# Attention backward on one core: transposing loads with 16 source rows instead of 32, and a third buffer for two stored tiles

## The chip, the cores and the metric

The kernel runs on one core of a Trainium2 chip. The metric is the time of one execution in microseconds (us) on the device. Single executions of one kernel spread by 1 to 2% here, so every comparison below is made on one chip, in alternating rounds. A quoted ratio is the mean time of one kernel's fast runs over that of the kernel before in the same rounds, so it is not quite the ratio of the medians that are quoted beside it. "Faster" means by more than 2%.

## The reference

Two independent attention blocks (A and B) and their gradients. For each block:

```
q      = (x @ wq) in 32 heads of 128            x: 8 x 96 x 640
scores = q k^T * 128^-0.5                       k_cache, v_cache: 8 x 32 x 512 x 128
p      = softmax(scores);  o = p v;  out = o @ wo
outputs: out of both blocks, and the gradients of x, k, v, wq, wo of each
```

Everything is bf16. The large tensors are K, V and their gradients dK, dV: per batch element and pair of heads, 256 KB each.

## The kernel before

The work is cut into 256 batch steps: 2 blocks x 16 head pairs x 8 batch elements. Each step needs K and V in two layouts, so it loads them twice: once plainly (V2, K2) and once transposed by the DMA (KT2, VT2), with the head dimension on the partitions. It stores dV and dK. That is six DMAs of 256 KB per step, all issued in program order by SP (the SyncE).

```python
def ldKT(hp, b):                                     # ldVT is alike, from vc, as VT2
    t_ = kvp.tile([128, RG, 32], BF16, name="KT2", bufs=3)            # RG = 512 / 16
    nc.sync.dma_start_transpose(t_[:], kc[b, 2*hp:2*hp+2].rearrange("h (r g) d -> (h r) (g d)", r=16))
...
def key_order(ap):   # the order of keys that the transpose leaves -> the order of the plain tiles
    return ap.rearrange("q (s c r) -> q c r s", c=KC, r=16)           # KC = 4
...
# cS: scores of head i. cDP does the same with VT into dP_ps.
nc.tensor.matmul(S_ps[:, i, :], hs["QT"][:, i, tok], st["KT"][:, :, i*16:(i+1)*16], start=True, stop=True)
...
# cE reads S_ps through key_order (exp, ACT); cDP's last step reads dP_ps so (DVE)
...
# cDV; cDK is alike with dS, Qnat, dK_sb, dk
... 8 matmuls into v_ps (one PSUM buffer, shared by cDV and cDK)
o = wk.tile([128, 2, KC * 128], BF16, name="dV_sb", bufs=2)
evac("act", o[:], v_ps[:])                                            # line 68, on ACT
nc.sync.dma_start(dv[b, 2*hp:2*hp+2].rearrange("h (p c) d -> p h (c d)", c=KC), o[:])
```

With `r=16` the source of a transpose is 32 rows (16 per head) of 8 KB. The rest of the work of a head pair (projections, dwq, dwo, dx) is spread over the steps.

Of the kernel before, what the change touches and what calls it, by code (L numbers as in the profile page):

```python
# [11 lines left out]
BF16 = mybir.dt.bfloat16  # L12
# [22 lines left out]
def build_block(tc, em, tick0, blk, x, kc, vc, wq, wo, g_all, out_all, dx, dk, dv, dwq, dwo, ident, ones, pools, first, GP):  # L35
    nc = tc.nc
# [6 lines left out]
    KC = Sk // 128  # L43
# [7 lines left out]
    RG = Sk // 16  # L51
# [8 lines left out]
    const, ps, psS, psV, kvp, wk, hd, hst, stp = (pools[k] for k in ("const", "ps", "psS", "psV", "kv", "wk", "hd", "hst", "stp"))  # L60
    S, G, HS, CS = {}, {}, {}, {}

    def bank(shape, dt, name):
        return ps.tile(shape, dt, name=name, tag="bank")

    def evac(eng, dst, src, sc=None):
        if eng == "act":
            nc.scalar.activation(dst, src, ACT.Identity, scale=(1.0 if sc is None else sc))  # L68
        elif sc is None:
            nc.vector.tensor_copy(dst, src)  # L70
        else:
            nc.vector.tensor_scalar(dst, src, float(sc), None, op0=ALU.mult)
# [98 lines left out]

    def ldKT(hp, b):
        def f():
            t_ = kvp.tile([128, RG, 32], BF16, name="KT2", bufs=3)
            nc.sync.dma_start_transpose(t_[:], kc[b, 2 * hp:2 * hp + 2].rearrange("h (r g) d -> (h r) (g d)", r=16))
            CS[(hp, b)] = dict(KT=t_)
        return f

    def ldVT(hp, b):
        def f():  # L180
            t_ = kvp.tile([128, RG, 32], BF16, name="VT2", bufs=3)
            nc.sync.dma_start_transpose(t_[:], vc[b, 2 * hp:2 * hp + 2].rearrange("h (r g) d -> (h r) (g d)", r=16))
            CS[(hp, b)]["VT"] = t_
        return f

# [12 lines left out]
        return f  # L198

    def key_order(ap):  # L200
        return ap.rearrange("q (s c r) -> q c r s", c=KC, r=16)

    def c_major(ap):
        return ap.rearrange("q (c r s) -> q c r s", c=KC, r=16)

    def cS(hp, b):
        def f():
            st, hs = CS[(hp, b)], HS[hp]
            tok = slice(b * Sq, (b + 1) * Sq)
            S_ps = psS.tile([Sq, 2, Sk], F32, name="S_ps", bufs=1)  # L210
            for i in range(2):
                nc.tensor.matmul(S_ps[:, i, :], hs["QT"][:, i, tok], st["KT"][:, :, i * 16:(i + 1) * 16], start=True, stop=True)  # L212
            negm = wk.tile([Sq, 2], F32, name="negm", bufs=2)
            nc.vector.tensor_reduce(negm[:], S_ps[:], axis=AX.X, op=ALU.max, negate=True)  # L214
            st["S_ps"], st["negm"] = S_ps, negm
        return f

    def cE(hp, b):
        def f():
            st = CS[(hp, b)]  # L220
            E = wk.tile([Sq, 2, Sk], BF16, name="E_sb", bufs=2)
            rowsum = wk.tile([Sq, 2], F32, name="rowsum", bufs=2)
            for i in range(2):
                nc.scalar.activation(c_major(E[:, i, :]), key_order(st["S_ps"][:, i, :]), ACT.Exp, bias=st["negm"][:, i:i + 1], scale=1.0, accum_out=rowsum[:, i:i + 1])  # L224
            st["E"], st["rowsum"] = E, rowsum
        return f
# [30 lines left out]
    def cDV(hp, b):  # L257
        def f():
            st, hs = CS[(hp, b)], HS[hp]
            v_ps = psV.tile([128, 2, KC * 128], F32, name="v_ps", bufs=1)  # L260
            for i in range(2):
                for c in range(KC):
                    nc.tensor.matmul(v_ps[:, i, c * 128:(c + 1) * 128], st["P"][:, i, c * 128:(c + 1) * 128], hs["dOnat"][:, i, b * 128:(b + 1) * 128], start=True, stop=True)  # L263
            o = wk.tile([128, 2, KC * 128], BF16, name="dV_sb", bufs=2)
            evac("act", o[:], v_ps[:])
            nc.sync.dma_start(dv[b, 2 * hp:2 * hp + 2].rearrange("h (p c) d -> p h (c d)", c=KC), o[:])
        return f
# [23 lines left out]
    def cDP(hp, b):  # L291
        def f():
            st, hs = CS[(hp, b)], HS[hp]
            tok = slice(b * Sq, (b + 1) * Sq)
            dS = wk.tile([Sq, 2, Sk], BF16, name="dS_sb", bufs=2)
            dl_ps = bank([Sq, 2], F32, "dl_ps")
            dps = []
            for i in range(2):
                dP_ps = bank([Sq, Sk], F32, "dP_ps")
                nc.tensor.matmul(dP_ps[:], hs["dOT"][:, i, tok], st["VT"][:, :, i * 16:(i + 1) * 16], start=True, stop=True)  # L300
                nc.tensor.matmul(dl_ps[:, i:i + 1], st["prod"][:, i, :], ones[:, 0:1], start=True, stop=True)  # L301
                dps.append(dP_ps)
            for i in range(2):
                nc.vector.scalar_tensor_tensor(c_major(dS[:, i, :]), key_order(dps[i][:]), dl_ps[:, i:i + 1], c_major(st["P"][:, i, :]), op0=ALU.subtract, op1=ALU.mult)  # L304
            st["dS"] = dS
        return f
# [13 lines left out]
    def cDK(hp, b):  # L320
        def f():
            st, hs = CS[(hp, b)], HS[hp]
            v_ps = psV.tile([128, 2, KC * 128], F32, name="v_ps", bufs=1)
            for i in range(2):
                for c in range(KC):
                    nc.tensor.matmul(v_ps[:, i, c * 128:(c + 1) * 128], st["dS"][:, i, c * 128:(c + 1) * 128], hs["Qnat"][:, i, b * 128:(b + 1) * 128], start=True, stop=True)  # L326
            o = wk.tile([128, 2, KC * 128], BF16, name="dK_sb", bufs=2)
            evac("act", o[:], v_ps[:])
            nc.sync.dma_start(dk[b, 2 * hp:2 * hp + 2].rearrange("h (p c) d -> p h (c d)", c=KC), o[:])
        return f  # L330
# [254 lines left out]
```

## Time and profile before

| | before |
|---|---|
| median of the first 3 runs | 1821.9 us (1809.4 to 1822.78) |
| profiled execution | 1809.5 us |
| PE busy | 1647.6 us, 91% |
| time with at least 15 DMA packets in flight (packet records, 100 to 1700 us) | 95% |
| eviction of dV_sb to the issue of its store, median | 6.1 us |

The list of waits of the kernel before: who waited for whom, us in total, times, longest.

```profile
ACT dV_sb L68 <- DMA out_dram<-dV_sb: 86.0, 47, 8.0
...
ACT dK_sb L68 <- DMA out_dram<-dK_sb: 25.3, 17, 4.7
...
PE v_ps L326 <- ACT dV_sb L68: 96.9, 88, 8.0
```

A store has not landed; ACT cannot evict into its buffer; PE cannot reuse v_ps. It is the only large wait on PE.

Two groups that read through `key_order` (busy us, mean ns of one | idle before, releaser):

```profile
L224 ACT ACTIVATE E_sb<-S_ps,negm 96x512 bf16<-96x512 f32 x512 | 346.0, 681 | 186.8 <-DVE negm L214 184.6
...
L304 DVE SCALAR_TENSOR_TENSOR dS_sb<-dP_ps,dl_ps,P_sb 96x512 bf16<-96x512 f32 x512 | 361.3, 744 | 120.2 <-PE dl_ps L301 119.7
```

### The profile page before, as it was taken

How to read it: one execution, taken by the hardware profiler on the slowest of the kernel's cores; microseconds unless marked ns; L12 is line 12 of the kernel's file. 1: busy time of each engine (PE TensorE's matmuls, PEld its weight loads, DVE VectorE, ACT ScalarE, POOL GpSimd, SP SyncE). 2: the span in 40 equal slices, each digit the busy share in tenths (PEclk: the TensorE clock that was granted, in tenths of full speed). 3: DMA queues.
4: the chain of work that ended last, by engine and by line, in shares of the span. 5: the costliest groups of instructions: out<-in, count | busy, mean ns of one | idle time of the engine just before them, and what ended most of it. 6: DMA issues, size and time to landing. Idle time of an engine off the chain costs nothing. (4 is left out here: it accounts for less than half of the span.)

```text
span 1809.5 us, 51178 instructions
## 1 busy us (share of the span) xinstructions
PE 1647.6 (91%) x20061; PEld 1264.4 (70%) x20280; DVE 1244.8 (69%) x2069; ACT 1185.7 (66%) x2433; POOL 615.2 (34%) x930
## 2 busy tenths in 40 slices
PE   6889989988999999999978989899898998999998
PEld 4667767766777777677756767667676776777775
DVE  3767776766776776666756667666676776777774
ACT  3766666766676766666756667667676766776673
POOL 2333333332333333333334433233332333333333
PEclk9999999999999999999999999999999999999999
DMA  9999999999999999999999999999999999999995
GB/s 237 256 277 271 273 247 282 264 267 253 260 281 259 275 281 262 250 258 276 272 264 259 277 271 267 267 245 254 278 281 259 269 255 275 280 285 279 253 295 171
DMA packets 918002, 478.82 MB, mean 265 GB/s; under 512 B 643040, under 2 KB 906720, under 8 KB 917760
## 3 DMA queue, kind: packets, MB, share of 16 engines
q1 hardware_dynamic: 904224, 425.73, 103.0%
q0 software_dynamic: 13536, 49.82, 9.1%
q8 instruction: 158, 2.59, 0.6%
q14 instruction: 84, 0.69, 0.1%
HBM read 161.09 MB, written 159.12 MB: 177 GB/s over the span
## 5 line engine op out<-in xcount | busy, mean ns | idle before, releaser
L241 POOL TENSOR_SCALAR P_sb<-E_sb,rinv 96x512 bf16<-96x512 bf16 x512 | 348.4, 690 | 499.1 <-DVE rinv L232 496.4
L224 ACT ACTIVATE E_sb<-S_ps,negm 96x512 bf16<-96x512 f32 x512 | 346.0, 681 | 186.8 <-DVE negm L214 184.6
L304 DVE SCALAR_TENSOR_TENSOR dS_sb<-dP_ps,dl_ps,P_sb 96x512 bf16<-96x512 f32 x512 | 361.3, 744 | 120.2 <-PE dl_ps L301 119.7
L214 DVE TENSOR_REDUCE negm<-S_ps 96x2 f32<-96x1024 f32 x256 | 311.7, 1217 | 104.8 <-PE S_ps L212 104.5
L68 ACT ACTIVATE dK_sb<-v_ps 128x1024 bf16<-128x1024 f32 x256 | 261.9, 1023 | 122.2 <-PE v_ps L326 69.8
L68 ACT ACTIVATE dV_sb<-v_ps 128x1024 bf16<-128x1024 f32 x256 | 261.7, 1022 | 119.8 <-DMA out_dram<-dV_sb 86.0
L287 POOL TENSOR_TENSOR prod<-OT,dOT 128x192 bf16<-128x192 bf16 x256 | 140.1, 547 | 527.4 <-ACT OT L68 517.4
L326 PE MATMUL v_ps<-Qnat,dS_sb 96*128 96x128 bf16 x2048 | 171.1, 223 | 100.2 <-ACT dV_sb L68 96.9
L326 PEld LDWEIGHTS <-dS_sb 96*128 96x128 bf16 x2048 | 138.7, 99 | 82.4 <-issue 57.8
L316 DVE COPY dST_sb<-dst_ps 128x768 bf16<-128x768 bf16 x256 | 140.5, 549 | 40.0 <-PE dst_ps L314 39.5
L263 PE MATMUL v_ps<-dOnat,P_sb 96*128 96x128 bf16 x2048 | 157.8, 220 | 1.5 <-ACT dK_sb L68 1.3
L390 PEld LDWEIGHTS <-x_nat 128*128 128x128 bf16 x960 | 93.6, 103 | 81.7 <-issue 63.1
L251 PEld LDWEIGHTS <-P_sb 96*128 96x128 bf16 x2048 | 113.5, 98 | 47.1 <-POOL P_sb L241 2.5
L253 DVE COPY PT_sb<-pt_ps 128x768 bf16<-128x768 bf16 x256 | 139.6, 545 | 4.6 <-PE pt_ps L251 4.4
L314 PEld LDWEIGHTS <-dS_sb 96*128 96x128 bf16 x2048 | 115.7, 98 | 33.8 <-issue 8.2
L390 PE MATMUL dwq_ps<-dQnat,x_nat 128*128 128x256 bf16 x960 | 132.8, 290 | 1.0 <-DVE dQnat L70 1.0
L314 PE MATMUL dst_ps<-ident,dS_sb 96*128 96x96 bf16 x2048 | 129.9, 206 | 2.5 <-ACT OT L68 0.8
L251 PE MATMUL pt_ps<-ident,P_sb 96*128 96x96 bf16 x2048 | 130.5, 206 | 1.4 <-POOL P_sb L241 1.0
L263 PEld LDWEIGHTS <-P_sb 96*128 96x128 bf16 x2048 | 123.3, 98 | 2.5 <-issue 2.2
L428 PE MATMUL o_ps<-wo_r,OT 128*128 128x128 bf16 (+1 forms) x691 | 120.4, 293 | 5.0 <-issue 1.1
L428 PE MATMUL o_ps<-wqT,dQT 128*128 128x128 bf16 (+1 forms) x692 | 118.5, 292 | 4.5 <-issue 0.7
L68 ACT ACTIVATE dwq_sb<-dwq_ps 128x512 bf16<-128x512 f32 (+1 forms) x96 | 50.5, 526 | 85.6 <-PE dwq_ps L390 83.0
(1606 smaller groups left out, 2937.3 us busy)
## 6 DMA issues: line engine op xcount, KB each, us to landing
out_dram<-dV_sb SPq DMA_DIRECT2D x256, 256.0 KB, 4.0
out_dram<-dK_sb SPq DMA_DIRECT2D x256, 256.0 KB, 4.6
out_dram<-dwo_sb POOLq DMA_DIRECT2D x32, 320.0 KB, 4.8
out_dram<-dwq_sb POOLq DMA_DIRECT2D x32, 320.0 KB, 5.7
wq_h<-in_A_wq_dram POOLq DMA_DIRECT2D x16, 320.0 KB, 6.1
wo_r<-in_A_wo_dram POOLq DMA_DIRECT2D x8, 640.0 KB, 7.0
wq_h<-in_B_wq_dram POOLq DMA_DIRECT2D x16, 320.0 KB, 7.2
wo_r<-in_B_wo_dram POOLq DMA_DIRECT2D x8, 640.0 KB, 6.7
```

What stands on the lines that cost most here:

```text
L68: nc.scalar.activation(dst, src, ACT.Identity, scale=(1.0 if sc is None else sc))
L214: nc.vector.tensor_reduce(negm[:], S_ps[:], axis=AX.X, op=ALU.max, negate=True)
L224: nc.scalar.activation(c_major(E[:, i, :]), key_order(st["S_ps"][:, i, :]), ACT.Exp, bias=st["negm"][:, i:i + 1], scale=1.0, accum_out=row ...
L241: nc.gpsimd.tensor_scalar(P2[:, i, :], st["E"][:, i, :], st["rinv"][:, i:i + 1], 0.0, op0=ALU.mult, op1=ALU.add)
L251: nc.tensor.transpose(pt[:, i, c, :], st["P"][:, i, c * 128:(c + 1) * 128], ident[0:Sq, 0:Sq])
L263: nc.tensor.matmul(v_ps[:, i, c * 128:(c + 1) * 128], st["P"][:, i, c * 128:(c + 1) * 128], hs["dOnat"][:, i, b * 128:(b + 1) * 128], star ...
L304: nc.vector.scalar_tensor_tensor(c_major(dS[:, i, :]), key_order(dps[i][:]), dl_ps[:, i:i + 1], c_major(st["P"][:, i, :]), op0=ALU.subtrac ...
L314: nc.tensor.transpose(t_ps[:, i, c, :], st["dS"][:, i, c * 128:(c + 1) * 128], ident[0:Sq, 0:Sq])
L316: nc.vector.tensor_copy(dST[:], t_ps[:])
L326: nc.tensor.matmul(v_ps[:, i, c * 128:(c + 1) * 128], st["dS"][:, i, c * 128:(c + 1) * 128], hs["Qnat"][:, i, b * 128:(b + 1) * 128], star ...
L390: nc.tensor.matmul(w_ps[:, j, :], S["x_nat"][:, t, (c0 + j) * 128:(c0 + j + 1) * 128], st["dQnat"][:, t, :, :], start=(t == 0), stop=(t == ...
L428: nc.tensor.matmul(o_ps[:, j, :], src[:, hh % 2, t_ * 128:(t_ + 1) * 128], w[:, hh, c0:c0 + wd], start=(hh == 0), stop=(hh == 2 * GP - 1))
```

## The change

Two things at once. The transposing loads see the same contiguous 256 KB as 16 rows of 16 KB (8 rows per head). And dV_sb and dK_sb get a third buffer.

```diff
-            t_ = kvp.tile([128, RG, 32], BF16, name="KT2", bufs=3)
-            nc.sync.dma_start_transpose(t_[:], kc[b, 2 * hp:2 * hp + 2].rearrange("h (r g) d -> (h r) (g d)", r=16))
+            t_ = kvp.tile([128, 2 * RG, 16], BF16, name="KT2", bufs=3)
+            nc.sync.dma_start_transpose(t_[:], kc[b, 2 * hp:2 * hp + 2].rearrange("h (r g) d -> (h r) (g d)", r=8))
 ... VT2 alike; key_order and c_major with r=8 ...
-                nc.tensor.matmul(S_ps[:, i, :], hs["QT"][:, i, tok], st["KT"][:, :, i * 16:(i + 1) * 16], start=True, stop=True)
+                nc.tensor.matmul(S_ps[:, i, :], hs["QT"][:, i, tok], st["KT"][:, :, i * 8:(i + 1) * 8], start=True, stop=True)
 ... VT alike ...
-            o = wk.tile([128, 2, KC * 128], BF16, name="dV_sb", bufs=2)
+            o = wk.tile([128, 2, KC * 128], BF16, name="dV_sb", bufs=3)
 ... dK_sb alike ...
```

More of the change, by code (lines that the diff above doesn't have):

```diff
@@ L180, in f @@
         def f():
-            t_ = kvp.tile([128, RG, 32], BF16, name="VT2", bufs=3)
-            nc.sync.dma_start_transpose(t_[:], vc[b, 2 * hp:2 * hp + 2].rearrange("h (r g) d -> (h r) (g d)", r=16))
+            t_ = kvp.tile([128, 2 * RG, 16], BF16, name="VT2", bufs=3)
+            nc.sync.dma_start_transpose(t_[:], vc[b, 2 * hp:2 * hp + 2].rearrange("h (r g) d -> (h r) (g d)", r=8))
             CS[(hp, b)]["VT"] = t_
@@ L200, in key_order @@
     def key_order(ap):
-        return ap.rearrange("q (s c r) -> q c r s", c=KC, r=16)
+        return ap.rearrange("q (s c r) -> q c r s", c=KC, r=8)
     def c_major(ap):
-        return ap.rearrange("q (c r s) -> q c r s", c=KC, r=16)
+        return ap.rearrange("q (c r s) -> q c r s", c=KC, r=8)
     def cS(hp, b):
@@ L299, in f @@
                 dP_ps = bank([Sq, Sk], F32, "dP_ps")
-                nc.tensor.matmul(dP_ps[:], hs["dOT"][:, i, tok], st["VT"][:, :, i * 16:(i + 1) * 16], start=True, stop=True)
+                nc.tensor.matmul(dP_ps[:], hs["dOT"][:, i, tok], st["VT"][:, :, i * 8:(i + 1) * 8], start=True, stop=True)
                 nc.tensor.matmul(dl_ps[:, i:i + 1], st["prod"][:, i, :], ones[:, 0:1], start=True, stop=True)
@@ L326, in f @@
                     nc.tensor.matmul(v_ps[:, i, c * 128:(c + 1) * 128], st["dS"][:, i, c * 128:(c + 1) * 128], hs["Qnat"][:, i, b * 128:(b + 1) * 128], start=True, stop=True)
-            o = wk.tile([128, 2, KC * 128], BF16, name="dK_sb", bufs=2)
+            o = wk.tile([128, 2, KC * 128], BF16, name="dK_sb", bufs=3)
             evac("act", o[:], v_ps[:])
```

## The prediction

> **What bounds it now.** The busy table has PE at 91% of 1809.5 us (1647.6 us); DVE 69%, ACT 66%. In the trace's packet records at least 15 packets are in flight 95% of the time: about 5% real idle.
>
> PE idles about 160 us. In the list of waits its only large item is v_ps (dK matmuls) waiting for the ACT eviction of dV_sb: 96.9 us, 88 times. ACT is late because dV_sb waits for the store of an older dV_sb, 86.0 us (47 times, up to 8.0 us), and dK_sb likewise, 25.3 us (17 times). A store is issued a median 6.1 us after its eviction (SP issues in order, and waits some 700 us for PE to free KT and VT buffers), then takes 4.0 us to land. With two buffers and a period of 6.5 us (median distance of dV evictions) that sometimes fails.
>
> **Why stores land late.** By the packet records a 256 KB transpose takes 14.4 ns per 256 B packet and engine when undisturbed (0.92 us), but on average 1.68 us. Some 310 times all engines stop about 30 packets into a transpose until a lagging engine catches up: 302 us in all, 215 us of it near a 16 KB instruction-fetch packet (about 1 us on one engine). woT and wqT, of other shapes, stop at the same place.
>
> **What the change does.**
> 1. Third buffer for dV_sb and dK_sb: a store gets one more period, 6.5 us, to land. Nearly all waits are shorter, so ACT's 111 us and PE's 97 us should almost vanish. DMA's idle share caps the gain near 90 us; some waits will move to loads. I expect 50 to 75 us.
> 2. 16 rows of 16 KB. A transpose stays 1024 packets of 256 B; each engine reads one contiguous row instead of alternating between two. The Trainium skill, "DMA: Bandwidth & Descriptors", section "Latency and other measured facts", gives a DMA transpose 261 GB/s with a non-contiguous middle dimension, 350 to 400 contiguous; this trace's undisturbed ones run at 290 GB/s. But woT, with rows far apart, has the same 14.4 ns, so I expect 14.4 ns and the same stops: 0 us most likely, with a small chance of 0.2 us per transpose (estimate from the page's rates), 100 us of DMA time.
> 3. The key order reads PSUM in runs of 16 instead of 8: ACT's exp (681 ns, against 589 for a plain 512-column eviction) and DVE's dS (744 ns) may lose up to 50 ns each, off the critical path: 0 to 10 us. PE's S and dP operands come in chunks of 8 elements instead of 16; I expect 385 ns unchanged.
>
> **Predicted: 1748 us, 80% range 1705 to 1800.** Faster by over 2%: 0.75; within 2%: 0.22; slower by over 2%: 0.03.
>
> **What would show it.** Step 1: waits of dV_sb and dK_sb on stores under 20 us, PE's v_ps wait under 25 us, PE 93 to 95% busy. Step 2: still 14.4 ns per packet and about 300 us of stops. Step 3: exp under 681 ns; matmuls L212, L300 unchanged.
>
> **What would make it wrong.** DMA is the true limit and the freed waits return as PE waiting for KT, VT, V or K (within 2%); contiguous rows speed up transposes or remove the stops (below 1705); 16-byte chunks slow the matmuls, or 16 KB rows slow the reads (slower).

## More of the kernel before

From the page of the kernel before: busy time of each engine (us, share of the span, instructions), the DMA packets of the whole run, and the two main DMA queues (packets, MB, packet time as a share of 16 engines' span; q1 carries what SP issues, q0 what POOL issues).

```profile
PE 1647.6 (91%) x20061; PEld 1264.4 (70%) x20280; DVE 1244.8 (69%) x2069; ACT 1185.7 (66%) x2433; POOL 615.2 (34%) x930
...
DMA packets 918002, 478.82 MB, mean 265 GB/s; under 512 B 643040, under 2 KB 906720, under 8 KB 917760
...
q1 hardware_dynamic: 904224, 425.73, 103.0%
q0 software_dynamic: 13536, 49.82, 9.1%
```

PE is nearly always busy, but so are the DMA engines: the times of their packets add up to more than the span (packet records overlap in time). Note the 643,040 packets under 512 B; the transposes' packets are of 256 B.

The timeline of SP in the kernel before (start, duration, the DMA issued):

```profile
799.16 1.28 SPq L182 DMA_TRANSPOSE VT_14978<-in_A_v_cache_dram  x1
800.54 0.53 SPq L266 DMA_DIRECT2D out_dram<-dV_sb  x1
801.17 0.42 SPq L329 DMA_DIRECT2D out_dram<-dK_sb  x1
801.68 1.74 SPq L175 DMA_TRANSPOSE KT_15254<-in_A_k_cache_dram  x1
```

SP issues one DMA after another without a real gap. Its 1586 issues add up to 1616 us of 1809.5. That can mean that issuing is slow, or that SP is held back because the DMA engines are behind.

## The result

The changed kernel takes 1750.1 us median (1744.59 to 1760.77, 4 runs) against 1820.02 us; the ratio of the fast runs is 0.9633, with a 95% interval of 0.9573 to 0.9694. It is faster, and 2.1 us from the forecast.

The page of the changed kernel, the same lines:

```profile
PE 1635.4 (93%) x20061; PEld 1257.6 (71%) x20280; DVE 1245.0 (71%) x2069; ACT 1183.3 (67%) x2433; POOL 612.9 (35%) x930
...
DMA packets 401906, 478.82 MB, mean 272 GB/s; under 512 B 118752, under 2 KB 382432, under 8 KB 393472
...
q1 hardware_dynamic: 388128, 425.73, 92.9%
q0 software_dynamic: 13536, 49.82, 8.5%
```

The bytes are the same, but there are 516,096 packets fewer. That is 512 transposes x (1024 - 16): a transpose that was 1024 packets of 256 B is now 16 packets side by side, which fits one per DMA engine (the packet records that were kept name no engine). The packet records of the two runs, tallied:

```
                       before                      after
KT/VT packets          1024 x 256 B                16 x 16384 B per transpose
undisturbed            14.4 ns per packet and      0.73 us per packet
                       engine, 0.92 us in all
whole transpose, 5th   0.94 us                     0.78 us   (first packet's start to last one's end)
  percentile
mean per transpose     1.68 us                     1.51 us
>= 15 in flight        95%                         93%
dV eviction to issue   6.1 us                      10.1 us   (median)
```

The waits of the changed kernel on the stores, and on PE:

```profile
ACT dV_sb L68 <- DMA out_dram<-dV_sb: 3.3, 7, 0.9
...
ACT dK_sb L68 <- DMA out_dram<-dK_sb: 2.7, 4, 0.8
...
PE S_ps L212 <- DMA KT_17757<-in_B_k_cache_dram: 5.3, 1, 5.3
PE S_ps L212 <- DMA KT_30653<-in_B_k_cache_dram: 5.1, 1, 5.1
PE S_ps L212 <- DMA KT_11217<-in_A_k_cache_dram: 4.7, 1, 4.7
PE v_ps L326 <- ACT dV_sb L68: 4.6, 29, 0.2
```

The old waits are gone, as forecast. But a new one is there: PE waits for KT, 30 times and 56 us in total (the list has one line per tile; three are shown). In the kernel before PE did not wait for KT.

The two groups with `key_order`:

```profile
L224 ACT ACTIVATE E_sb<-S_ps,negm 96x512 bf16<-96x512 f32 x512 | 345.8, 681 | 209.0 <-DVE negm L214 208.1
L304 DVE SCALAR_TENSOR_TENSOR dS_sb<-dP_ps,dl_ps,P_sb 96x512 bf16<-96x512 f32 x512 | 363.5, 745 | 166.3 <-PE dl_ps L301 117.3
```

Neither changed: 681 and 681 ns, 744 and 745 ns.

So the profile already doubts the forecast's account. Theory A (the prediction): the third buffer gives the gain. Theory B: the shorter transposes give it, and the third buffer only moved a wait.

### The profile page after: what moved, and what is told of

Its sections match the earlier page's. It is cut to its first block, busy times and chain, and to the rows that moved or that the text cites. A ratio compares the mean times of both kernels' runs of the same rounds, so it can differ in the third digit from the quotient of the medians.

```text
span 1759.0 us, 51176 instructions
## 1 busy us (share of the span) xinstructions
PE 1635.4 (93%) x20061; PEld 1257.6 (71%) x20280; DVE 1245.0 (71%) x2069; ACT 1183.3 (67%) x2433; POOL 612.9 (35%) x930
## 3 DMA queue, kind: packets, MB, share of 16 engines
q1 hardware_dynamic: 388128, 425.73, 92.9%
## 4 chain that ended last, share of the span: by engine, by line
PE 67%; DMA 16%; ACT 7%; DVE 5%; issue 4%; POOL 1%; SPq 0%; POOLq 0%; ACTq 0%; DVEq 0%
PE o_ps L428 8%; PE q_ps L149 6%; PE dwq_ps L390 6%; PE v_ps L326 6%; PE S_ps L212 5%; PE dq_ps L341 5%; PE dP_ps L300 4%; PE v_ps L263 4%; PE dwo_ps L370 4%; PE dst_ps L314 4%; PE ot_ps L278 4%; ACT dV_sb L68 3%; PE pt_ps L251 3%; ACT E_sb L224 3%; DVE negm L214 2%
```

## The experiments

Twelve runs were made; run 10 is the changed kernel once more. All gave correct results. A run counts as slow when it is over 1.5% above the fastest of the same kernel; only fast runs enter the ratios.

### 1 and 2: each half of the change alone

`e1_bufs_only` is the kernel before with `bufs=3` for dV_sb and dK_sb:

```diff
-            o = wk.tile([128, 2, KC * 128], BF16, name="dV_sb", bufs=2)
+            o = wk.tile([128, 2, KC * 128], BF16, name="dV_sb", bufs=3)      # dK_sb alike
```

> Third buffer for dV_sb and dK_sb, transposes of before (32 rows of 8 KB). Theory A (the prediction: the buffer gives the gain, the rows nothing): 1745 to 1765 us, ratio about 0.963, waits of dV_sb and dK_sb on their stores under 20 us. Theory B (the rows give most of it, because an undisturbed transpose fell from 0.92 to about 0.75 us): 1795 to 1815 us, and the waits on the stores come back as PE waiting for KT and K.

`e2_rows_only` is the changed kernel with `bufs=2` for both:

```diff
-            o = wk.tile([128, 2, KC * 128], BF16, name="dV_sb", bufs=3)
+            o = wk.tile([128, 2, KC * 128], BF16, name="dV_sb", bufs=2)      # dK_sb alike
```

> 16 rows of 16 KB, two buffers for dV_sb and dK_sb as in before. Theory A: 1810 to 1825 us, dV_sb and dK_sb still wait about 110 us for their stores. Theory B: 1755 to 1775 us, since stores land earlier behind shorter transposes, and these waits fall below 50 us. If each gives about half, both runs lie near 1785 us.

Measured: the buffers alone 1834.51 us, ratio 1.0103 (1.0024 to 1.0182). The rows alone 1755.17 us, ratio 0.9665 (0.9591 to 0.974). Theory A falls: the whole gain is in the rows. The buffers alone came out slower even than theory B expected (1795 to 1815 us). Runs 9 and 10 repeat the rows alone and the full change. Waits with the buffers alone:

```profile
ACT dV_sb L68 <- DMA out_dram<-dV_sb: 16.2, 11, 6.8
...
PE S_ps L212 <- DMA KT<-in_B_k_cache_dram: 51.8, 21, 8.5
PE S_ps L212 <- DMA KT<-in_A_k_cache_dram: 39.4, 19, 7.4
PE dq_ps L341 <- DMA K<-in_B_k_cache_dram: 16.0, 12, 3.9
```

and with the rows alone:

```profile
ACT dV_sb L68 <- DMA out_dram<-dV_sb: 54.2, 36, 5.5
ACT dK_sb L68 <- DMA out_dram<-dK_sb: 18.5, 19, 2.1
...
PE v_ps L326 <- ACT dV_sb L68: 63.0, 78, 5.5
```

With the third buffer 94 of the 111 us of waits on stores went away, and 91 us of waiting for KT came in their place. Nothing was won, and the DMA engines were just as full (at least 15 packets in flight 95% of the time) with the same work to do. The store's lag fits this: with a third buffer ACT evicts without waiting, the queue in front of the DMA engines simply grows (median 11.6 us from eviction to issue, against 6.1), and the loads in that queue come late instead. The kernel with the rows alone is as fast as the full change although 73 us of waits on stores are still in it. Theory B foresaw that they would fall below 50 us, so on that point its expectation missed too.

### 3: more buffers for the new wait

```diff
-            t_ = kvp.tile([128, 2 * RG, 16], BF16, name="KT2", bufs=3)
+            t_ = kvp.tile([128, 2 * RG, 16], BF16, name="KT2", bufs=4)       # VT2 alike
```

> The changed kernel with four buffers instead of three for KT2 and VT2. In the changed kernel PE waits 56 us for KT (30 times), new against before. If that is a lack of buffers: the wait falls under 15 us and the time to 1700 to 1725 us. If it is DMA throughput (at least 15 packets in flight 93% of the time): 1740 to 1760 us, and the wait stays or moves to other loads.

Measured: 1792.7 us, ratio 0.9868 (0.9806 to 0.993), some 40 us slower than the changed kernel. The waits:

```profile
PE v_ps L326 <- ACT dV_sb L68: 42.9, 68, 6.2
PE dq_ps L341 <- DMA K<-in_B_k_cache_dram: 30.1, 26, 4.8
PE dq_ps L341 <- DMA K<-in_A_k_cache_dram: 20.4, 22, 2.4
```

The wait for KT is gone from PE's list, and waits for K and for the stores stand in its place. That a wait only moves agrees with DMA throughput as the limit; that the kernel got slower was foreseen by neither reading. With four buffers SP's program issues KT and VT earlier, ahead of stores and K loads (a store now leaves SP 13.0 us after its eviction, against 10.1), and at least 15 packets are in flight only 90% of the time, against 93%. That the early transposes push urgent transfers back is argued from this, not shown by a run of its own.

### 4: one transpose per head

Two transposes of 16 rows of 8 KB in place of one, with three store buffers.

```diff
-            nc.sync.dma_start_transpose(t_[:], kc[b, 2 * hp:2 * hp + 2].rearrange("h (r g) d -> (h r) (g d)", r=16))
+            for i in range(2):
+                nc.sync.dma_start_transpose(t_[:, i], kc[b, 2 * hp + i].rearrange("(r g) d -> r (g d)", r=16))
```

> One transpose per head, 16 rows of 8 KB each, two in place of one; three buffers for dV_sb and dK_sb. If 16 source rows are what lets an engine move its row as one packet, the packet records show 8 KB packets (16 per transpose) of about 0.37 us undisturbed; if 16 KB rows are needed, 256 B packets. SP issues two more transposes per batch step (about 1.3 us each), so I expect it slower than the changed kernel: 1780 to 1950 us.

Measured: 2179.18 us, ratio 1.1986, slower than expected. The packet records have 16 packets of 8192 B per transpose, 0.31 us undisturbed. So it is not the 16 KB row that makes one packet of a row; 16 rows of 8 KB do it too, where 32 rows of 8 KB did not. The timeline of SP in this kernel:

```profile
1001.68 0.57 SPq L198 DMA_DIRECT2D K<-in_A_k_cache_dram  x1
1002.35 1.10 SPq L176 DMA_TRANSPOSE KT<-in_A_k_cache_dram  x1
1003.54 3.24 SPq L184 DMA_TRANSPOSE VT<-in_A_v_cache_dram  x2
1006.88 0.53 SPq L268 DMA_DIRECT2D out_dram<-dV_sb  x1
```

Here 1024 transposes of 128 KB cost SP at least 1.10 us each, as those of 256 KB do in the changed kernel; its issues add up to 1966 us of 2168.6, while at least 15 packets are in flight only 64% of the time. So in this kernel SP's issuing is most likely the bound. That raised a rival to DMA throughput (theory D) for the others too. Theory S: SP's issuing is the bound everywhere, and the rows pay because a transpose of 16 rows costs SP at least 1.10 us and one of 32 rows 1.27 us, some 85 us in 512.

### 5 and 6: the stores issued from ACT's queue

```diff
-            nc.sync.dma_start(dv[b, ...
+            nc.scalar.dma_start(dv[b, ...           # dk alike
```

On the kernel before:

> The kernel before (32 rows of 8 KB, two buffers), with the stores of dV and dK issued from ACT's queue instead of SP's; the DMA work is the same. Theory S (new: SP's issuing is the bound; in the profile of before its DMA issues take 1616 us and the short gaps between them most of the rest of 1809 us): SP loses 512 issues, 265 us, and the time falls to 1690 to 1740 us. Theory D (DMA throughput is the bound): 1790 to 1825 us.

On the changed kernel:

> The changed kernel with the stores of dV and dK issued from ACT's queue. Theory S: 1680 to 1720 us, near the bound that PE's 1635 busy us set, and hardly below the previous run, since the cheaper transposes no longer matter. Theory D: 1740 to 1755 us, and 60 us or more below the previous run.

Measured: 1819.9 us, ratio 0.9971 (0.9902 to 1.004), and 1770.78 us, ratio 0.9658 (0.959 to 0.9727). Both are against theory S. The DMA theory held for the first and missed for the second, which it had at 1740 to 1755 us and at least 60 us below the first; it was 49 us below. SP lost 512 issues, but did not become free: a KT issue of 32 rows now takes a median 2.09 us where it took 1.47. So much of SP's "issuing" is time in which it is held back. The rows still pay about 3% when SP issues 512 DMAs fewer. One reservation: the scheduler also reordered PE, DVE and ACT in these two, so they are not as clean as runs 11 and 12.

The Trainium skill, "DMA: Bandwidth & Descriptors", section "Issuing engines are not separate DMA queues", says that all issuing engines feed the same 16 DMA engines and that a second one only saves issue time. These two runs agree.

### 7 and 8: one extra small DMA per step, on 16 engines or on one

The tile of V2 gets a spare third, filled by an extra load of 16 or 17 rows of 1 KB that nobody reads.

```diff
-            t_ = kvp.tile([128, 2, KC, 128], BF16, name="V2", bufs=3)
+            t_ = kvp.tile([128, 3, KC, 128], BF16, name="V2", bufs=3)
 ... the load of V2 into t_[:, 0:2], then:
+            nc.sync.dma_start(t_[0:16, 2], vc[b, 2 * hp].rearrange("(p c) d -> p c d", c=KC)[0:16])     # or 17
```

> The changed kernel with one extra load per batch step from SP, 16 rows of 1 KB into an unused part of V's tile: one packet on each of the 16 engines, 1% more bytes. Theory S: SP issues 256 more, each 0.4 to 0.5 us with its gap: 1840 to 1890 us. Theory D: 1750 to 1775 us.

> As the run before, but 17 rows of 1 KB, which should go to one engine alone (17 has no divisor up to 16 but 1): 17 packets of about 45 ns on it, so that it lags by some 0.7 us while the others go on to a transpose. If one lagging engine stops all 16 in a transpose (read from the packet records only, so far) and the stops cost time: 60 to 150 us more than with 16 rows. If SP's issuing alone sets the time: within 20 us of it.

Measured: 1822.99 us with 16 rows, ratio 0.9967 (0.9912 to 1.0021), and 1849.9 us with 17 rows, ratio 1.0117 (1.0054 to 1.018). The first lies between the two theories: 1% more bytes cost some 3% (the changed kernel stood at 0.9633 and 0.968). A DMA has a price beyond its bytes; whether SP or the DMA engines pay it, this run does not tell.

The pair does tell something about lagging. The skill's page, section "Why a DMA increments its semaphore by 16 and not by 1", says that a DMA runs on the largest number of engines up to 16 that divides the slowest dimension of both its sides, so 17 rows run on one. The packet records agree: with 17 rows the extra DMAs leave 256 semaphore packets, with 16 rows 4096. Each puts some 0.77 us of packets (17 x 45 ns) on one engine. The price was 27 us, against 60 to 150 expected, and the transposes took 31 us longer in sum (814 against 783, each from its first packet's start to its last one's end). This agrees with a lagging engine that holds up transposes, at a price in time that is much less than the sum of the lags (256 x 0.77 us, 197 us).

### 9 and 10: the third buffer once more, in five rounds

The rows alone, and the changed kernel unaltered, side by side.

> The rows alone once more (two buffers), beside the changed kernel on one chip, to see what the third buffer adds to the rows. If the third buffer only moves the wait from the stores to KT: both within 10 us, near 1755 us, and waits on stores of some 70 us here. If it adds 20 us or more once the rows are cheaper: 1775 us against 1750 us.

> The changed kernel, unaltered, beside the previous run: 1745 to 1765 us. If the third buffer only moves the wait: within 10 us of the previous run, with 50 to 60 us of PE waiting for KT. If it adds to the rows: 20 us or more below it.

Measured: the rows alone 1752.99 us, ratio 0.9651 (0.9607 to 0.9695); the full change 1757.58 us, ratio 0.968 (0.9637 to 0.9724). Waits with the rows alone:

```profile
PE v_ps L326 <- ACT dV_sb L68: 68.1, 77, 6.0
```

and with the full change:

```profile
PE S_ps L212 <- DMA KT<-in_A_k_cache_dram: 30.4, 19, 4.3
PE S_ps L212 <- DMA KT<-in_B_k_cache_dram: 27.2, 19, 2.8
...
PE v_ps L326 <- ACT dV_sb L68: 6.0, 26, 1.8
```

With and without the third buffer the times agree within their intervals. The 68 us of one wait have become 58 us of another.

### 11 and 12: the stores issued from POOL's queue

```diff
-            nc.sync.dma_start(dv[b, ...
+            nc.gpsimd.dma_start(dv[b, ...           # dk alike
```

On the changed kernel:

> The changed kernel with the stores of dV and dK issued from POOL's queue; unlike the run with ACT's queue, the order on PE, DVE and ACT stays almost the same, and SP loses 512 issues of 0.5 us. Theory S (SP's issuing is the bound): 1690 to 1720 us. Theory D (DMA time is the bound): 1740 to 1775 us, with SP now showing real gaps.

Measured: 1686.47 us, ratio 0.9305 (0.9249 to 0.9362). This beats both kernels. The page and PE's waits:

```profile
PE 1626.4 (96%) x20280; PEld 1245.1 (74%) x20280; DVE 1243.7 (74%) x2069; ACT 1183.7 (70%) x2433; POOL 992.5 (59%) x1442
...
DMA packets 303602, 478.82 MB, mean 284 GB/s; under 512 B 118752, under 2 KB 251360, under 8 KB 295168
...
q1 hardware_dynamic: 248864, 291.48, 71.9%
q0 software_dynamic: 54496, 184.07, 30.3%
```

```profile
PE v_ps L326 <- ACT dV_sb L68: 8.9, 56, 0.2
...
PE S_ps L212 <- DMA KT<-in_B_k_cache_dram: 5.9, 3, 2.4
```

PE is at 96% and has hardly a wait left. The time is the one that theory S gave, just under its range. But there is a difference to ACT's queue that I had not thought of: POOL's queue writes the stores in packets of 4096 B (32,768 of them, in place of 131,072 of 1024 B). The skill's page, section "SWDGE vs HWDGE vs iDMA", says that a packet of this queue is preferably up to 4096 B (in this trace the same queue also carries 4480 packets of 5120 B). A 4096 B packet takes a median 165 ns here, four of 1024 B take 184 ns. The queues' packet time falls from 92.9% + 8.5% of 1759.0 us, 1784 us, to 71.9% + 30.3% of 1686.4 us, 1723 us: 60 us less. That is no measure of the gain, since packet records overlap: from the kernel before to the changed one it fell by 245 us, and the time by 50 us. That the larger packets are what makes POOL's queue pay is argued, not shown. So this run had relieved SP, and perhaps the DMA engines, at once. The last run tests whether SP's issuing is what the rows save: POOL's stores with the transposes of before. Its order on every engine is the same as in run 11.

```diff
-            t_ = kvp.tile([128, 2 * RG, 16], BF16, name="KT2", bufs=3)
+            t_ = kvp.tile([128, RG, 32], BF16, name="KT2", bufs=3)      # and VT2, key_order, c_major, S, dP as before
```

> As the run with the stores from POOL's queue (1686 us), but with the transposes of before (32 rows of 8 KB); the order on every engine is the same, so only the transposes' shape differs. If the rows pay through DMA time (0.92 against 0.74 us undisturbed, 90 us in 512 transposes) and DMA is still near its limit: 1740 to 1775 us, with PE waiting for KT again. If they pay through SP's issuing (1.27 against 1.10 us at least), SP has 512 issues fewer and is no longer the bound: 1680 to 1705 us. If POOL's stores took DMA off the critical path: also 1680 to 1705 us, but with DMA less full.

Measured: 1826.78 us (1796.09 to 1839.56). Only two of the four runs are fast, 1796.09 and 1816.22 us; the ratio of the fast runs is 0.9891 (0.9767 to 1.0015), which is unclear against 2%. Both fast runs lie above all three expected ranges, the 1740 to 1775 us of the DMA theory too. Against run 11 this kernel differs by the transposes' shape alone, and loses 6% (0.9891 against 0.9305), some 106 us. At their cheapest its SP issues would fill some 1000 us (an estimate: 512 transposes at 1.27 us, 512 loads at 0.42 us, and some 150 us for woT and wqT), so SP's own work is not the bound in it. Theory S, which gave 1680 to 1705 us, falls. What is left is DMA time; what within the DMA path makes 1024 small packets dearer than 16 large ones, no run separates. With three buffers and SP's stores the rows gave 0.042 to 0.047 (1.0103 against 0.968 and 0.9633); beside POOL's stores they gave 0.059, which the intervals do not clearly set apart.

One more thing differs between the kernels, the clock that PE was granted, as a share of its full speed. It was 0.963 to 0.965 in the runs with the buffers alone (run 1) and 0.981 to 0.985 in those with the rows alone (run 2). PE was busy 1676.0 us in the profile of run 1 and 1641.5 us in that of run 2, with the same 20280 matmuls: some 35 us of the 100 us between these two spans. So a part of the gap goes with the clock. Not all of it does: a run of the kernel before took 1806.28 us at a clock of 0.979, and one of the changed kernel 1758.93 us at 0.980. Why the clock differs, no run shows; it does not follow the rows alone, for runs 7 and 8 have 16 rows and stood at 0.966 to 0.971.

## Why the prediction was right or wrong

The number was right: 1748 us forecast, 1750.1 us measured. The account was not. Two terms of the sum were wrong by about the same amount in opposite directions, so the number was right by luck.

**Step 1, "I expect 50 to 75 us" from the third buffer: failed, it gave no gain.** Alone it measured 1.0103, and on top of the rows it made no difference that five rounds can see (0.968 with it, 0.9651 without). The step read an idle time of PE off the list of waits and took its removal for a gain. It named the check itself (at least 15 packets in flight 95% of the time) and read "5% real idle" as room for 90 us. The 5% never moved: with the third buffer alone it was 5% again. "DMA is the true limit and the freed waits return as PE waiting for KT, VT, V or K" stood in the list of what would make it wrong, and that is what happened to this half.

**Step 2, "0 us most likely" from the rows: failed, it gave all of it.** The packets did not stay 1024 of 256 B. The step argued from woT, whose rows lie far apart and whose packets take the same 14.4 ns, that contiguity does not matter. But all 606,208 packets of the transposes in the trace of before, woT's and wqT's included, are of 256 B: it held no transpose with packets of a whole row, so it could not decide. That an engine alternates between two rows when there are 32 is the prediction's reading, which the records, without engine numbers, do not show. The skill's figure could: section "Latency and other measured facts" gives 350 to 400 GB/s for contiguous transposes, and 16 x 16384 B in 0.73 us are 359 GB/s (338 GB/s over the 0.78 us of the whole transpose). Its 261 GB/s for the other case is somewhat below the 262144 B in 0.92 us, 285 GB/s, of this trace. The "small chance" term of 0.2 us per transpose and 100 us of DMA time was close in size: 0.92 - 0.73 us is 0.19 us (0.94 - 0.78 us is 0.16 us for whole transposes), and the mean fell from 1.68 to 1.51 us, 87 us in 512 transposes. The time fell by 55 to 75 us in the runs with the rows.

**"The same stops": not shown.** What a transpose takes beyond its undisturbed time is about as much as before: 1.68 - 0.92 = 0.76 us, and 1.51 - 0.73 = 0.78 us. But a packet of 16 KB does not show where inside it an engine stops, so whether these are the same stops is open.

**Step 3: right in effect, wrong in one check.** 0 to 10 us was expected; exp and dS did not change at all (681 and 745 ns), so "exp under 681 ns" failed. The S matmuls (L212) take a median 379 ns before and 382 ns after, and 379 ns in run 2, which has the same chunks; those of dP (L300) take 381 ns in all three. So chunks of 8 elements cost PE next to nothing.

**The checks of step 1 all passed** (waits on stores 6 us, PE's v_ps wait 4.6 us, PE 93%) although the step was false. They tested whether the waits would go, not whether the time would. A check on the sum of PE's waits would have caught it in the run with the buffers alone: 133 us before, and 151 us there.

## What to carry to other kernels

A wait that stands on a full queue is not worth its length: first ask whether the server behind the queue has room, because a further buffer for one customer only makes another wait. Count DMA packets, not only bytes: shape a transposing load so that it has 16 source rows, each contiguous, and see in the packet counts whether each row has become one packet (16 and 32 rows are all that was tried here, and two transposes in place of one cost more than they saved). When a change has two parts, run each alone even if the total came out as forecast.

## What the Trainium skill lacked or had wrong

- "DMA: Bandwidth & Descriptors", on DMA transpose: it has the two rates, a "non-contiguous mid-dim" and a "≥4KB-M2S-concat constraint", but not which source shape meets it. Here 16 source rows became one packet per row (16384 B in 0.73 us, 8192 B in 0.31 us), and 32 rows of the same 256 KB became 1024 packets of 256 B (14.4 ns each, 0.92 us).
- The same page, same subject: it does not say that one lagging engine holds up the others in a transpose. Here some 310 transposes of the kernel before stopped about 30 packets in, 302 us in all, 215 us of it near a 16 KB instruction fetch of about 1 us, by the author's count. A recount from the kept packet records, which name no engine, gives 270 to 295 transposes, some 280 us, and 140 to 180 us near a fetch. An added lag of some 0.77 us per step on one engine cost 27 us in all (run 8 against run 7).
- The same page, "Issuing engines are not separate DMA queues": "will only save the time on the sequencer" held for ACT's queue (0.9971), but not for POOL's. There the packets of a store grew from 1024 to 4096 B, and the time fell to 0.9305 of before where the same kernel without the move is at 0.968. Whether the larger packets are the reason, no run shows.
- The same page, in its part on another chip, gives 631 cycles of sequencer time for a DMA transpose of small tiles on "previous generations", and no figure in us for one of 256 KB: here SP needed at least 1.10 us for 16 rows of 8 or 16 KB, and 1.27 us for 32 rows of 8 KB, against 0.4 us for a plain 256 KB DMA.
